# Adding the residual x with accumulating transfers from GpSimd instead of VectorE, with a new order of all work

## The chip, the cores and the metric

The kernel runs on one core of a Trainium2 chip. A core has five engines with a queue of instructions each, and every queue is worked off strictly in its order: TensorE (PE in the profile, with its weight loads as PEld), VectorE (DVE), ScalarE (ACT), GpSimd (POOL) and SyncE (SP), which here only issues transfers between the chip's main memory and the on-chip memory. Engines wait for each other by semaphores. Products of matrices land in banks of a separate small memory (PSUM), from which VectorE and ScalarE take them.

The metric is the device time of one execution in microseconds. Three runs of the kernel before gave 566.79, 567.97 and 567.18 us, a median of 567.18 us. One further execution was recorded by the hardware profiler: it took 566.9 us, and its span, from the first to the last instruction, is 564.8 us.

## The reference

The input x has 2048 tokens of 512 numbers. All is in 32-bit floats, and the result is x + s * g.

```python
xn = layernorm(x)                       # over the 512, eps 1e-5
q, k, v = split(xn @ wqkv)              # 32 heads of 16
phi = lambda t: where(t > 0, t + 1, exp(t)) + 1e-6
kv = einsum("bhsd,bhse->bhde", phi(k), v); z = phi(k).sum(tokens)
o = (phi(q) @ kv) / (phi(q) @ z + 1e-6)
s = o @ wo                              # linear attention
h = gelu(xn @ w_gate) * (xn @ w_up)     # 512 -> 1792
g = silu(h @ w_down)                    # 1792 -> 512
return x + s * g
```

## The kernel before

**The result is made transposed.** Channels lie on the 128 partitions and tokens along the rows. The output is 512 channels by 2048 tokens, cut into four chunks `c` of 512 tokens and four row tiles `n` of 128 channels: 16 output tiles of 128x512, 256 KB each. `in_A_xT` is x in the same layout.

**Precision.** A 32-bit product is made from three faster ones: each operand is split into a high part (a rounded copy, made on ScalarE by `copy`) and a low part (the difference, made on VectorE or GpSimd; `split`, L406). Large products use a scheme of seven half-size products in place of eight (`PRODUCTS`, L180), whose partial sums are seeded and taken out between products (`copy` for seeds, `out` at L1111).

**Stages.** First the tokens are normalized and k, q and the attention's sums are made (to about 140 us). At the very start, SP loads x tiles (`x0`, `x4`, `x1`, `x5`) and halves of two weights (`wk1`, `wk2`); VectorE takes the mean and variance of a tile (L552, L553, L555), GpSimd the power -1/2 (`rstd`, L557), VectorE normalizes it (`xn`, L573), TensorE transposes it (`pt`, L643), ScalarE makes its high part (`Xh`), and the first product of the main work is `k<-kq,Xh`. The high parts of the weights (`kq<-wk`) are made on ScalarE; for the later half of each weight the low part is made on GpSimd.

Then the feed-forward part runs twice over half of the tokens, `ffn(1)` for chunks 2 and 3 and `ffn(0)` for chunks 0 and 1. Its products with w_gate and w_up are `FX`, `FY`, `FZ`, those with w_down `dX`, `dY`, `dZ`; the latter are summed by VectorE into `acc` (L1119). Low parts of w_down's forms are `dl`, and for the last of seven steps they are made on GpSimd (`EASED`).

**The output tiles** (`out_tile`, L1317). For each, the gate `g` is at hand: for chunks 0 and 1 it is `acc` after `silu` on ScalarE (L1346), for chunks 2 and 3 it was stored to main memory and is loaded again into one of ten places (`SPOTS`). It is multiplied by the attention's result `s` (L1335 from a bank `sps`, L404 where `s` was stored and is loaded again, as in chunk 2), then the tile of x is added, which SP has loaded into a place of its own (`sxr`, L1326 and L1338), and SP stores the sum to `out_yT`. The chunks come in the order 2, 3, 0, 1; the last tile of all, chunk 1 with n = 3, is done in two halves of 256 tokens.

**What sets the order.** Nothing is issued where it is written. `plan.do` records each operation with what it depends on, and the list `ORDER` at the head of the file gives one permutation of all 3626 operations. They are issued in this order, and it sets what stands ahead of what in each engine's queue; semaphores then keep what depends on each other apart. `ORDER` was written out by a planner that is not part of the file. Transfers that SP issues use eight semaphores in turn, so a ninth waits until the first has landed; a store waits for its tile, and all that stands behind a waiting instruction in a queue waits with it.

## Time and profile before

| | us |
|---|---|
| median of three runs | 567.18 (566.79 to 567.97) |
| profiled execution, its own time | 566.9 |
| its span | 564.8 |
| TensorE busy | 557.8 |
| VectorE busy | 493.2 |
| ScalarE busy | 360.8 |
| GpSimd busy | 253.1 |

The span is what the profiler's rows cover; 2.1 us of the execution lie outside it. Rows of a timeline give a start from the span's begin, a duration, the engine, the line and operation with its tiles, a count where equal ones are merged, and in brackets how long the engine had been idle and what released it. A single instruction lasts longer than its distance to the next, since instructions of an engine overlap a little. The granted clock of TensorE was 0.999 of full speed.

### The profile page before, as it was taken

To read this page: it belongs to the slowest core of one execution; us is meant where nothing else is said; L and a number is where in the kernel's file an instruction comes from. 1 tells how busy PE (TensorE), PEld (TensorE's weight loads), DVE (VectorE), ACT (ScalarE), POOL (GpSimd) and SP (SyncE) were. 2 spreads that over 40 slices of the span, in tenths; PEclk is the share of its full clock that TensorE was granted. 3 is DMA by queue.
4 is the path that set the end of the run, shared out by engine and by line. 5 is a ranking of instruction groups with operands and counts; after the bars stand their busy time and mean duration, and the time that the engine had idled before them with its cause. 6 is when DMAs were issued, how large, how long until landed. Compare 5 with 4: busy or idle time off the path is not lost.

```text
span 564.8 us, 7902 instructions
## 1 busy us (share of the span) xinstructions
PE 557.8 (99%) x2630; PEld 487.0 (86%) x2630; DVE 493.2 (87%) x774; ACT 360.8 (64%) x668; POOL 253.1 (45%) x237
## 2 busy tenths in 40 slices
PE   8999999999999999999999999999999999999997
PEld 6888888888888888888888888888888888888886
DVE  7999999987798999999888776774889989898997
ACT  5987898877677876564536467867555636354730
POOL 4656677757786876431251940430413212314200
PEclk9999999999999999999999999999999999999999
DMA  7378967879978668158867998696757475778776
GB/s 266 104 217 273 274 203 233 255 223 322 352 241 300 240 234 339 43 201 311 265 233 216 389 339 335 239 344 254 243 187 242 173 247 194 233 228 286 239 247 239
DMA packets 78952, 141.29 MB, mean 250 GB/s; under 512 B 4672, under 2 KB 47680, under 8 KB 74944
## 3 DMA queue, kind: packets, MB, share of 16 engines
q1 hardware_dynamic: 78912, 140.79, 72.9%
q8 instruction: 21, 0.34, 0.2%
q14 instruction: 19, 0.16, 0.1%
HBM read 87.82 MB, written 52.95 MB: 249 GB/s over the span
## 4 chain that ended last, share of the span: by engine, by line
PE 91%; DVE 5%; DMA 2%; issue 1%; SPq 1%; ACT 0%; DVEq 0%; ACTq 0%
PE FX L442 26%; PE FZ L442 13%; PE dX L442 12%; PE gps L442 7%; PE FY L442 6%; PE dY L442 6%; PE X L442 6%; PE sps L442 4%; PE dZ L442 3%; PE Z L442 3%; PE q L442 2%; PE k L442 2%; PE Y L442 1%; DVE acc L1119 1%; PE pt L643 1%; DMA wk<-in_A_wqkv 1%
## 5 line engine op out<-in xcount | busy, mean ns | idle before, releaser
L442 PE MATMUL FX<-Xh,w 128*128 128x512 f32 x448 | 125.4, 379 | 0.0
L442 PEld LDWEIGHTS FX<-Xh,w 128*128 128x128 f32 x448 | 84.7, 189 | 12.0
L404 POOL TENSOR_TENSOR sums<-draw 128x256 f32<-128x256 f32 x28 | 26.5, 951 | 109.6 <-DVE dl L404 56.3
L1165 POOL TENSOR_TENSOR h<-h,g 128x512 f32<-128x512 f32 x28 | 39.5, 1411 | 65.9 <-DVE h L404 64.2
L442 PE MATMUL FX<-Xl,w 128*128 128x512 f32 x224 | 66.0, 379 | 0.0
L442 PE MATMUL FZ<-Xh,w 128*128 128x512 f32 x224 | 64.4, 379 | 0.0
L398 ACT COPY dY<-dX 128x512 f32<-128x512 f32 x56 | 32.1, 573 | 46.2 <-DVE acc L1119 28.4
L398 ACT COPY fu<-FX 128x512 f32<-128x512 f32 x56 | 32.7, 585 | 23.3 <-PE FX L442 19.4
L442 PEld LDWEIGHTS FX<-Xl,w 128*128 128x128 f32 x224 | 42.3, 189 | 6.0
L442 PEld LDWEIGHTS FZ<-Xh,w 128*128 128x128 f32 x224 | 42.3, 189 | 6.0
L398 ACT CAST hfh<-sums 128x512 fp32r<-128x512 f32 x56 | 34.5, 619 | 14.3 <-DVE sums L404 14.3
L442 PE MATMUL dX<-hfh,dh 128*128 128x512 f32 x112 | 41.9, 380 | 0.1
L442 PE MATMUL dX<-hfl,dh 128*128 128x512 f32 x112 | 41.5, 380 | 0.0
L442 PE MATMUL dX<-hfh,dl 128*128 128x512 f32 x112 | 41.0, 379 | 0.0
L1119 DVE TENSOR_TENSOR acc<-acc,dY 128x512 f32<-128x512 f32 x48 | 32.7, 681 | 8.9 <-PE dY L442 8.7
L404 DVE TENSOR_TENSOR hfl<-sums,hfh 128x512 fp32r<-128x512 f32 x56 | 40.2, 728 | 0.1
L404 POOL TENSOR_TENSOR tmp<-raw 128x256 f32<-128x256 f32 x28 | 29.1, 1049 | 20.1 <-DVE we L404 10.6
L1119 DVE TENSOR_TENSOR acc<-acc,dX 128x512 f32<-128x512 f32 x48 | 32.7, 683 | 5.5 <-PE dX L442 5.2
L960 POOL TENSOR_TENSOR qz<-qz,zq 128x512 f32<-128x512 f32 x16 | 23.3, 1456 | 23.1 <-DMA qz<-q_d 18.3
L442 PE MATMUL FY<-Xh,w 128*128 128x512 f32 x112 | 33.1, 379 | 0.0
L442 PE MATMUL FZ<-Xl,w 128*128 128x512 f32 x112 | 33.0, 379 | 0.0
L404 DVE TENSOR_TENSOR hfl<-h,hfh 128x512 fp32r<-128x512 f32 x42 | 32.2, 774 | 0.6 <-ACT hfh L398 0.6
(222 smaller groups left out, 1517.7 us busy)
## 6 DMA issues: line engine op xcount, KB each, us to landing
w<-w_d SPq DMA_DIRECT2D x17, 1792.0 KB, 7.9
w_d<-w SPq DMA_DIRECT2D x11, 1792.0 KB, 8.8
draw<-in_B_w_down SPq DMA_DIRECT2D x14, 512.0 KB, 4.0
w_d<-we SPq DMA_DIRECT2D x18, 256.0 KB, 2.2
x<-in_A_x SPq DMA_DIRECT2D x16, 256.0 KB, 3.3
q_d<-qp SPq DMA_DIRECT2D x16, 256.0 KB, 3.7
qz<-q_d SPq DMA_DIRECT2D x16, 256.0 KB, 3.1
q<-q_d SPq DMA_DIRECT2D x16, 256.0 KB, 3.8
```

Source lines behind the costliest of these rows:

```text
L398: do("ACT", act(n, src.psum), lambda o, i: nc.scalar.copy(o, i), dst, src, name=name)
L404: do(eng, c, lambda o, p, q: getattr(e, f"tensor_{op}")(o, p, q), dst, a, b, name=name)
L442: nc.tensor.matmul(o if r is None else o[:, r], a, turned(b), start=first, stop=made == self.passes[r], skip_group_check=self.on or r is n ...
L643: nc.tensor.transpose(o[:, k, :], a[:, j * P:(j + 1) * P], b)
L960: do("POOL", pool(D), lambda o, z: nc.gpsimd.tensor_mul(o, o, z.unsqueeze(1).to_broadcast([P, KT, P])), rows_of(q), zq, name="u")
L1119: do("DVE", dve(D), lambda o, i: nc.vector.tensor_add(o, o, i), o, ps, name="acc")
L1165: do("POOL", pool(NC), lambda o, i: nc.gpsimd.tensor_mul(o, o, i), h, g, name="h")
```

## The change

For the 12 tiles of chunks 2, 3 and 0 the load of x by SP and the addition by VectorE are gone. After the multiplication GpSimd issues a transfer with `accum_op=ALU.add`, which reads the tile of x from main memory and adds it to the tile `g` in place; SP's store waits for it. Chunk 1 is left as it was. So VectorE has 12 instructions fewer, SP 12 loads fewer, GpSimd 12 transfers more, and TensorE's products and ScalarE's work are the same in number: 2602 and 670 rows with merged ones counted apart, in both. The places `SPOTS` now hold only gates and `s`. `ORDER` is another list throughout, of 3614 operations. Lines of the changed kernel stand one lower up to L1323, and seven or eight higher behind the new lines.

```diff
 ORDER = [
-    ...
+    ...
 ]
@@ def out_tile(c, n, ps):
             else:
                 g = U("g", SPOTS, f"g{c}{n}")
                 dma(g, g_d(4 * (c - 2) + n, at(c - 2, n)), 256)
+            if c in ADDED:
+                if ps.psum:
+                    do("DVE", dve(NC), lambda o, i: nc.vector.tensor_mul(o, o, i), g, ps)
+                else:
+                    tt("DVE", "mul", g, g, ps, NC)
+                do("POOL", 1.0, lambda o, i: nc.gpsimd.dma_start(o, i, accum_op=ALU.add), g, ext(xT[rows, cols]), lat=2.6, kb=256, name="add")
+                dma(ext(outT[rows, cols]), g, 256)
+                return
             xr = U(*(("xr", FREED) if c == CHUNKS[-1] else ("g", SPOTS)), f"sxr{c}{n}")
             dma(xr, ext(xT[rows, cols]), 256)
@@
     CHUNKS = [2, 3, 0, 1]
+    ADDED = (2, 3, 0)
```

Three places of the order are shown. Names end in a running number of the buffer; what stands ahead of it is the program's name (`sps03`: chunk 0, n = 3; `acc0_1`: the tile that holds n = 2 and n = 3 of chunk 0; `acc0_2` and `acc0_3`: chunk 1; `x4` is the second tile that is normalized).

SP's queue at its very begin, before:

```order
L394 DMA x0_97<-in_A_x 128x512
L394 DMA wk1_113<-in_A_wqkv 128x512
L394 DMA wk2_119<-in_A_wqkv 128x512
L394 DMA x4_121<-in_A_x 128x512
L394 DMA x1_123<-in_A_x 128x512
L394 DMA x5_125<-in_A_x 128x512
L394 DMA wk2_119<-in_A_wqkv 128x512
L394 DMA wk1_113<-in_A_wqkv 128x512
```

The same place of SP's queue now:

```order
L393 DMA wk1_98<-in_A_wqkv 128x512
L393 DMA x0_119<-in_A_x 128x512
L393 DMA x1_121<-in_A_x 128x512
L393 DMA wk2_123<-in_A_wqkv 128x512
L393 DMA x4_125<-in_A_x 128x512
L393 DMA x5_127<-in_A_x 128x512
L393 DMA wk2_123<-in_A_wqkv 128x512
L393 DMA wk1_98<-in_A_wqkv 128x512
```

The first tile of x comes second instead of first, behind a weight tile, and the first tile of `wk2` fourth instead of third; the seventh and eighth loads are the same. In GpSimd's queue the subtraction for that weight tile now stands ahead of the first `rstd`; before, it stood behind it.

The end of GpSimd's queue, before:

```order
L404 TENSOR_TENSOR sums0_3878<-draw0_6_5230,sums0_3878 128x256
L404 TENSOR_TENSOR dl0_6_5442<-draw0_6_5230,dh0_6_5431 128x512
L404 TENSOR_TENSOR dl3_6_5467<-sums0_3878,dh3_6_5459 128x512
L404 TENSOR_TENSOR dl5_6_5486<-sums0_3878,dh5_6_5476 128x512
L404 TENSOR_TENSOR dl2_6_5538<-draw0_6_5230,dh2_6_5533 128x256
```

The end of GpSimd's queue now, but for its last six rows:

```order
L1329 DMA g21_5460<-in_A_xT 128x512
L403 TENSOR_TENSOR dl3_6_5524<-sums0_3853,dh3_6_5515 128x512
L403 TENSOR_TENSOR dl5_6_5536<-sums0_3853,dh5_6_5531 128x512
L403 TENSOR_TENSOR dl2_6_5562<-draw0_6_5245,dh2_6_5555 128x256
L1329 DMA g32_5486<-in_A_xT 128x512
L1329 DMA g30_5497<-in_A_xT 128x512
L1329 DMA g23_5418<-in_A_xT 128x512
L1329 DMA g22_5578<-in_A_xT 128x512
```

Behind these stand six more accumulating transfers; the last of all is that of `acc0_1` for chunk 0, n = 3. Two (`g20`, `g21`) stand ahead of the `dl3`, `dl5` and `dl2` that TensorE needs.

The end of VectorE's queue, before:

```order
L1335 TENSOR_TENSOR acc0_2_4124<-acc0_2_4124,sps11_5753 128x512
L404 TENSOR_TENSOR acc0_1_4195<-acc0_1_4195,sxr03_5696 128x512
L404 TENSOR_TENSOR acc0_2_4124<-acc0_2_4124,sxr11_5740 128x512
L404 TENSOR_TENSOR acc0_0_4080<-acc0_0_4080,sxr00_5718 128x512
L1335 TENSOR_TENSOR acc0_3_4142<-acc0_3_4142,sps12_5774 128x512
L404 TENSOR_TENSOR acc0_3_4142<-acc0_3_4142,sxr12_5690 128x512
L1335 TENSOR_TENSOR acc0_2_4124<-acc0_2_4124,sps10_5675 128x512
L404 TENSOR_TENSOR acc0_2_4124<-acc0_2_4124,sxr10_5750 128x512
L1333 TENSOR_TENSOR acc0_3_4142<-acc0_3_4142,sps131_5800 128x256
L404 TENSOR_TENSOR acc0_3_4142<-acc0_3_4142,sxr13_5645 128x256
L1333 TENSOR_TENSOR acc0_3_4142<-acc0_3_4142,sps130_5812 128x256
L404 TENSOR_TENSOR acc0_3_4142<-acc0_3_4142,sxr13_5645 128x256
```

The end of VectorE's queue now:

```order
L1340 TENSOR_TENSOR acc0_3_4187<-acc0_3_4187,sps130_5741 128x256
L1118 TENSOR_TENSOR acc0_1_4223<-acc0_1_4223,dX06_1_5633 128x512
L1342 TENSOR_TENSOR acc0_2_4170<-acc0_2_4170,sps11_5693 128x512
L1326 TENSOR_TENSOR acc0_1_4223<-acc0_1_4223,sps03_5593 128x512
L403 TENSOR_TENSOR acc0_2_4170<-acc0_2_4170,sxr11_5747 128x512
L403 TENSOR_TENSOR acc0_3_4187<-acc0_3_4187,sxr13_5675 128x256
L1342 TENSOR_TENSOR acc0_3_4187<-acc0_3_4187,sps12_5725 128x512
L403 TENSOR_TENSOR acc0_3_4187<-acc0_3_4187,sxr12_5553 128x512
L1342 TENSOR_TENSOR acc0_2_4170<-acc0_2_4170,sps10_5779 128x512
L403 TENSOR_TENSOR acc0_2_4170<-acc0_2_4170,sxr10_5714 128x512
L1340 TENSOR_TENSOR acc0_3_4187<-acc0_3_4187,sps131_5799 128x256
L403 TENSOR_TENSOR acc0_3_4187<-acc0_3_4187,sxr13_5675 128x256
```

The last stores in SP's queue, before:

```order
L394 DMA out_yT<-acc0_0_4080 128x512
L394 DMA out_yT<-acc0_1_4195 128x512 x2
L394 DMA out_yT<-acc0_2_4124 128x512
L394 DMA out_yT<-acc0_0_4080 128x512
L394 DMA out_yT<-acc0_3_4142 128x512
L394 DMA out_yT<-acc0_2_4124 128x512
L394 DMA out_yT<-acc0_3_4142 128x256 x2
```

The last stores in SP's queue now:

```order
L393 DMA out_yT<-acc0_0_4091 128x512
L393 DMA out_yT<-acc0_2_4170 128x512
L393 DMA out_yT<-acc0_3_4187 128x256
L393 DMA out_yT<-acc0_3_4187 128x512
L393 DMA out_yT<-acc0_1_4223 128x512
L393 DMA out_yT<-acc0_2_4170 128x512
L393 DMA out_yT<-acc0_3_4187 128x256
```

The multiplication for chunk 0, n = 3 (`sps03`) stands fourth of the last twelve on VectorE, right behind the last sum into that tile (`dX06_1`). Its store is the third from the end in SP's queue and now waits for the accumulating transfer; before, those four tiles of chunk 0 were finished by VectorE. On TensorE, 24 products of 512 columns and 16 of 256 now stand behind the last of `dX06_1`, and 20 and 12 behind the last of `sps11`.

287 rows, old and new, of the table ORDER are left out of this document.

## The prediction

> **What bounds the kernel now.** I read the page first (span, busy times, slices, chain), then the table of stretches, then the timelines of both ends.
>
> ```profile
> span 564.8 us, 7902 instructions
> PE 557.8 (99%) x2630; PEld 487.0 (86%) x2630; DVE 493.2 (87%) x774; ACT 360.8 (64%) x668; POOL 253.1 (45%) x237
> PE 91%; DVE 5%; DMA 2%; issue 1%; SPq 1%; ACT 0%; DVEq 0%; ACTq 0%
> ```
>
> The chain of waits is TensorE's for 91%. VectorE has 5%, all near the end, so an edit that unloads VectorE there looks well aimed. But a chain follows one of several tight paths; whether TensorE would end sooner without VectorE is seen only in its idle time, by stretch.
>
> ```profile
> 0.00:40.00 40.00, 37.24 (x185) 31.91 (x186) 35.18 (x69) 30.43 (x57) 23.71 (x30) 1.00 0.63 199
> 40.00:80.00 40.00, 39.97 (x197) 34.57 (x196) 37.83 (x67) 32.59 (x62) 25.22 (x23) 1.00 0.85 255
> 80.00:120.00 40.00, 40.00 (x187) 35.00 (x187) 38.39 (x58) 35.72 (x68) 29.34 (x27) 1.00 0.74 228
> ...
> 200.00:240.00 40.00, 39.91 (x185) 34.65 (x184) 38.45 (x58) 24.64 (x48) 25.15 (x25) 1.00 0.58 214
> ...
> 280.00:320.00 40.00, 39.86 (x185) 34.39 (x184) 33.46 (x53) 21.45 (x40) 21.30 (x17) 1.00 0.77 275
> ...
> 520.00:540.00 20.00, 20.00 (x94) 17.50 (x94) 19.11 (x31) 13.81 (x25) 4.41 (x4) 1.00 0.79 260
> 540.00:565.00 25.00, 20.86 (x109) 18.41 (x107) 21.51 (x37) 4.10 (x7) 0.00 (x0) 0.98 0.69 239
> ```
>
> First column after the length: TensorE's busy time, third: VectorE's. The stretches left out have 40.00. From 40 to 540 us TensorE idles 0.03 + 0.09 + 0.14 = 0.26 us, and from 540 it works without a gap until 560.86. VectorE is close behind it (19.11 of 20). Since the change leaves TensorE's products as they are, only three things can move: the start, what little stalls there are or will be between, and the 564.8 - 560.86 = 3.9 us behind the last product.
>
> **The change part by part. Removed from VectorE.**
>
> ```profile
> L404 DVE TENSOR_TENSOR g<-g,sxr 128x512 f32<-128x512 f32 x8 | 5.3, 687 | 0.0
> 548.06 1.90 DVE L404 TENSOR_TENSOR g<-g,sxr 128x512 f32<-128x512 f32 x3
> 549.17 1.89 PE L442 MATMUL sps<-pql,Mh 128*128 128x512 f32 x8
> ```
>
> Three additions take 1.90 us and each lasts 0.69, so they follow each other by (1.90 - 0.69) / 2 = 0.60. Twelve are 12 x 0.60 = 7.2 us of VectorE's last 50. TensorE covers them: it has no gap here to give back. The value of the removal is therefore 0, and the part of the 3.9 us that depends on it is looked at next. From the third row, eight products in 1.89, each lasting 0.38: one every 0.216 us.
>
> **The last 3.9 us.**
>
> ```profile
> 558.91 1.95 PE L442 MATMUL sps<-pqh,Mh 128*128 128x256 f32 x16
> 560.01 0.41 DVE L1333 TENSOR_TENSOR acc<-acc,sps 128x256 f32<-128x256 f32 x1
> 560.46 0.42 DVE L404 TENSOR_TENSOR acc<-acc,sxr 128x256 f32<-128x256 f32 x1
> 560.90 0.42 DVE L1333 TENSOR_TENSOR acc<-acc,sps 128x256 f32<-128x256 f32 x1
> 561.35 0.42 DVE L404 TENSOR_TENSOR acc<-acc,sxr 128x256 f32<-128x256 f32 x1
> 553.77 8.37 SPq L394 DMA_DIRECT2D out_yT<-acc  x9
> ```
>
> The last multiplication starts 0.04 us behind the last product, so VectorE is not late any more when TensorE ends: multiply, add, store (561.77 to the end) is a fixed chain, and it stays, as chunk 1 is not edited. With E the end of the last product, the last store is issued at about E + 0.9.
>
> What is new is the store ahead of it. SP now issues, as its last three, the store of chunk 0 n = 3, which waits for the last accumulating transfer, and then two of chunk 1. When is that transfer issued? Behind `dX06_1` stand 24 full and 16 half products: 24 x 0.216 + 16 x 0.108 = 6.9 us before E. On VectorE `sps130` comes first (its products end 0.43 later; it takes 0.41), so the sum into the tile runs from E - 6.0 to E - 5.4; then ScalarE's silu:
>
> ```profile
> 552.57 0.63 ACT L1346 ACTIVATE acc<-acc 128x512 f32<-128x512 f32 x1 [0.57 <-DVE acc L1119]
> sxr<-in_A_xT SPq DMA_DIRECT2D x5, 256.0 KB, 3.2
> out_yT<-acc SPq DMA_DIRECT2D x7, 256.0 KB, 2.6
> DMA to landing us min/median/max: 2.8/3.7/7.7
> DMA packets 78952, 141.29 MB, mean 250 GB/s; under 512 B 4672, under 2 KB 47680, under 8 KB 74944
> ```
>
> Silu ends at about E - 4.65 and the multiplication by `sps03`, 0.68 long, at E - 3.95. Let L be the time from there until the sum has landed. SP then issues three stores, 0.45 apart (nine with waits took 8.37; the three loads at the start below took 1.39): the last at E - 3.95 + L + 0.9. It is late if that is over E + 0.9, so for **L above 3.95 us**, and by as much as L is above it. No row shows such a transfer. Below, L cannot be better than a plain store near the end, 2.6; above, I take the slowest load of x, 7.7 (last row but one: all 16). The nearest row is the load of x in the last 20 us, 3.2; the sum also reads its destination, another 262 KB, which at the mean of 250 GB/s is 1.05 us. 3.2 + 1.05 = 4.25: the end moves by **0.3** (0 to 3.75).
>
> The Trainium skill, "DMA: Bandwidth & Descriptors", section on the anatomy of a transfer on the GpSimd path, gives 2.0 us plus bytes / 436 GB/s, and about 1 us more to write the descriptors: an estimate of 1.0 + 2.0 + 0.6 = 3.6 us. By it this term is 0 and the sum below is lower by 0.3; no run here shows it yet.
>
> The other eleven have room: the first two matter most. `g20`'s place is loaded anew with `g33`, behind accumulation, store and load; counted as above, `g20` is multiplied by E - 35.5 and `g33` is used at E - 17.4, so 18 us less a store and a load (3.9 median for `g`'s, twice) leave 10 for L.
>
> **GpSimd's queue.** `g20` and `g21` stand ahead of three low parts that TensorE needs.
>
> ```profile
> 522.06 3.24 POOL L404 TENSOR_TENSOR dl<-sums,dh 128x512 fp32r<-128x512 f32 x2 [1.95 <-ACT dh L398]
> L394 SPq DMA_DIRECT2D g<-g_d x8: 319/423/430, 510.7 to 538.5; - x8
> DMA to landing us min/median/max: 2.3/3.9/5.6
> ```
>
> `g21`'s multiplication ends by E - 33.7; even if GpSimd needs a whole 1.6 us, as for one of these subtractions, to issue it, `dl3` is ready at E - 30.5, and its product stands at E - 26.5. Hidden with 4 us to spare.
>
> **The start.** A new order begins with another order of loads.
>
> ```profile
> 2.17 1.39 SPq L394 DMA_DIRECT2D x<-in_A_x  x3
> 3.42 0.69 DVE L552 BATCH_NORM_STATS2 st<-x 128x6 f32<-128x512 f32 x1 [2.36 <-DMA x<-in_A_x]
> 4.22 0.62 ACT L398 CAST kq<-wk 128x512 fp32r<-128x512 f32 x1 [2.15 <-DMA wk<-in_A_wqkv]
> 4.60 0.56 POOL L557 TENSOR_TENSOR rstd<-ve,neg_half 128x1 f32<-128x1 f32 x1 [2.27 <-DVE ve L555]
> 5.12 2.68 POOL L404 TENSOR_TENSOR kq<-wk,kq 128x512 fp32r<-128x512 f32 x2
> 5.19 1.48 DVE L573 TENSOR_SCALAR xn<-x,mv,rstd 128x512 f32<-128x512 f32 x1 [0.68 <-POOL rstd L557]
> 5.42 0.62 ACT L398 CAST kq<-wk 128x512 fp32r<-128x512 f32 x1 [0.58 <-DMA wk<-in_A_wqkv]
> 6.73 0.66 PE L643 MATMUL pt<-blk,xn 128*128 128x128 f32 x4 [1.25 <-DVE xn L573]
> 7.94 1.16 PE L442 MATMUL k<-kq,Xh 128*128 128x512 f32 x4
> 8.68 1.31 ACT L398 CAST kq<-wk 128x512 fp32r<-128x512 f32 x2 [0.61 <-DMA wk<-in_A_wqkv]
> 9.28 0.54 DVE L573 TENSOR_SCALAR xn<-x,mv,rstd 128x512 f32<-128x512 f32 x1
> 9.35 0.48 PE L442 MATMUL k<-kq,Xh 128*128 128x512 f32 x1 [0.25 <-ACT kq L398]
> ```
>
> Before, the first loads land at 3.42, 4.22 and 5.42. Now the weight tile has 3.42 and x 4.22, 0.8 later. `rstd` was due 4.60 - 3.42 = 1.18 behind x: now 5.40. GpSimd's subtraction for the weight stands ahead of it, from 3.42 + 0.62 = 4.04 to 4.04 + 1.34 = 5.38: no wait. `rstd` ends at 5.96. Before, the normalization lasted 1.48, as GpSimd's subtraction ran beside it; alone it lasts 0.54 (at 9.28). Now the second subtraction waits for a tile that comes fourth, behind 5.42, and its cast, so the normalization runs alone and ends at about 6.6, as before (6.67). So the 0.8 is paid back by the collision that goes, and the first product stays near 7.9. The seventh load, for which TensorE waits until 9.35, is the same. Behind it ScalarE has a copy between its two casts (0.55 later), and TensorE fills part of that with transposes brought forward (0.41 each): **+0.2**, between -0.5 (both waits there, 0.25 each, go) and +0.8 (the swap is not paid back).
>
> **Between.** No gain above 0.26 is there. A loss is open: VectorE is busy 38.4 of 40 us in two of the stretches above, and one instruction put ahead of one that TensorE waits for costs 0.60. Four such places would be 2.4, none 0. Before has under half of one in 500 us, so I take **+0.3**, the size of what it has, between -0.3 and +2.4.
>
> **Sum,** against the profiled execution: 566.9 + 0.3 + 0.2 + 0.3 = 567.7. The median of the runs is 0.28 above that execution, so **568.0 us**: no change, where 0.2% (1.1 us) is about what a measurement of this kernel tells from none.
>
> **The rivals.** *A busier order stalls TensorE (slower).* For it: VectorE at 96% in the middle, and 0.26 us of gaps is a state with little left to improve and much to lose. Against: VectorE's work there is no more than before. With three or four places of 0.60, 1.8 to 2.4 in place of 0.3: 569.5 to 570.
>
> *The last accumulating transfer is slow (slower).* Place: third store from the end of SP's queue; from L = 3.95 each microsecond is one of the end. For it: loads of x took up to 7.7. Against: few transfers are left at that time. At 7.7, 568.0 - 0.3 + 3.75 = 571.4. The Trainium skill, "SBUF — State Buffer", section on the two sides, warns that descriptor writing on GpSimd starves while VectorE runs in its two-port mode, 620 ns becoming some 3100; it names copies, and the rows here are TENSOR_TENSOR, which no run here has shown beside such a transfer.
>
> *VectorE did hold the end (faster).* For it: the chain names VectorE from 541 on. Against: TensorE has no gap there. What can be won in all is the waits at the start (1.25 and 0.25) and the 0.26 between: 567.2 - 1.8 = 565.4.
>
> That the change doesn't do what it says is excluded by the order: 12 transfers stand on GpSimd and 12 additions are missing on VectorE.
>
> **How the numbers follow.** No change, 50%; stalls between, 25%; a late landing, 13%; faster, 12%. The forecast's own range is 566.1 to 568.3. Eight in ten needs most of the stalls and no more than the edge of the rest: 566.2 to 570.6. Faster by over 0.2% is the last rival alone, 0.12; slower the two slow ones, 0.38; within 0.2% 0.50.
>
> **What would show it.** Right: TensorE's busy time within 0.5 of 557.8, no idle stretch over 0.5 behind 16 us, the first `k` product between 7.4 and 8.7, VectorE's busy time near 493 - 12 x 0.68 = 485, and the last store issued 0.9 behind the last product or up to 0.3 later. Wrong: a wait of TensorE for VectorE or GpSimd of 0.6 or more between 16 and 560 us, or SP waiting at the third store from the end for over 0.5 us behind E. A span that shrinks by over 1.1 us would show a slack at the start that I don't see.

## The result, and the profile after

The changed kernel takes **570.97 us** (median; 569.78 to 571.38) against 567.33 us (566.79 to 567.97) of the kernel before, run beside it: a ratio of 1.0059, 95% interval 1.0043 to 1.0075. It is slower by 0.6%, three times what a measurement of this kernel can tell. The profiled execution took 570.96 us, its span is 569.1, 4.3 more than before.

The page of the changed kernel, first lines and shares of the chain of waits:

```profile
span 569.1 us, 7898 instructions
PE 558.8 (98%) x2630; PEld 488.0 (86%) x2630; DVE 494.1 (87%) x762; ACT 361.5 (64%) x668; POOL 259.1 (46%) x249
PE 88%; DVE 5%; DMA 4%; issue 1%; ACT 0%; SPq 0%; POOL 0%; DVEq 0%; ACTq 0%; POOLq 0%
```

VectorE has 12 instructions fewer and is as busy as before. TensorE's share of the chain fell by 3 points and that of the DMA engines doubled. The last product ends at 562.66 in place of 560.86, and behind it the span goes on for 6.44 us in place of 3.94. So 1.8 us are lost while TensorE still has work, and 2.5 us behind it.

**The middle.** The stretches of the changed kernel (after the length: busy time of TensorE, its weight loads, VectorE, ScalarE, GpSimd; then the granted clock, the share of the 16 DMA engines, GB/s), and the groups of TensorE's instructions between 16 and 560 us that waited for 0.3 us or more:

```profile
200.00:240.00 40.00, 40.00 (x187) 35.04 (x186) 38.00 (x57) 24.94 (x50) 25.81 (x25) 1.00 0.46 176
240.00:280.00 40.00, 39.36 (x183) 34.12 (x181) 38.06 (x62) 23.28 (x43) 6.32 (x6) 1.00 0.67 237
280.00:320.00 40.00, 38.83 (x176) 33.01 (x177) 34.67 (x49) 18.97 (x36) 22.01 (x18) 1.00 0.77 267
320.00:360.00 40.00, 40.00 (x187) 35.01 (x187) 28.27 (x44) 21.87 (x40) 13.45 (x14) 1.00 0.91 353
L441 PE MATMUL FZ<-Xh,w 128*128 128x512 f32 x224 | 65.1, 379 | 0.9 <-DMA w<-w_d 0.9
L441 PE MATMUL dX<-hfl,dh 128*128 128x512 f32 x112 | 41.1, 380 | 0.5 <-DVE hfl L403 0.5
L441 PE MATMUL dY<-hfh,dh 128*128 128x512 f32 x56 | 21.3, 381 | 0.3 <-ACT dY L397 0.3
```

Up to 240 us the new order is even a little better: by 254 us TensorE is 0.54 us ahead of the kernel before. Then it waits for a weight tile (at 279 us), for a low part from VectorE (285) and for a copy by ScalarE (295), and all of it is some 250 us ahead of the first accumulating transfer. SP's queue in that place, now and before:

```profile
269.62 0.43 SPq L393 DMA_DIRECT2D t_d<-sums  x1
270.15 0.44 SPq L393 DMA_DIRECT2D w<-w_d  x1
275.09 0.32 SPq L393 DMA_DIRECT2D q<-q_d  x1
```

```profile
264.53 1.16 SPq L394 DMA_DIRECT2D t_d<-sums  x1
265.80 0.58 SPq L394 DMA_DIRECT2D w<-w_d  x1
272.54 0.32 SPq L394 DMA_DIRECT2D q<-q_d  x1
```

The weight tile that TensorE waits for (`w12`) is asked for 4.35 us later than before, as it stands behind q loads and t stores of the turning steps, which VectorE does about 6 us later in the new order (the first transposition of the second half at 263.24 in place of 257.23).

**The tail.** The changed kernel: the last transfer in the chain of waits, VectorE and SP near the end, GpSimd's last transfer, and the DMA queues and issues between 525 and 572 us (MB, share of 16 engines; median us to landing):

```profile
554.69 7.01 DMA sxr<-in_A_xT
557.97 0.69 DVE L1326 TENSOR_TENSOR acc<-acc,sps 128x512 f32<-128x512 f32 x1
561.80 1.03 DVE L403 TENSOR_TENSOR acc<-acc,sxr 128x512 f32<-128x512 f32 x2 [3.15 <-DMA sxr<-in_A_xT]
565.84 0.42 DVE L403 TENSOR_TENSOR acc<-acc,sxr 128x256 f32<-128x256 f32 x1
553.70 2.09 SPq L393 DMA_DIRECT2D sxr<-in_A_xT  x2
559.06 0.89 POOL L1329 DMA_DIRECT2D acc<-in_A_xT  x1 [5.13 <-DVE acc L1326]
q0 software_dynamic: 1728, 3.15, 39.3%
g<-in_A_xT POOLq DMA_DIRECT2D x8, 256.0 KB, 6.1
sxr<-in_A_xT SPq DMA_DIRECT2D x4, 256.0 KB, 6.9
acc<-in_A_xT POOLq DMA_DIRECT2D x4, 256.0 KB, 6.1
```

VectorE waits 3.15 us for the last x tile of chunk 1 (`sxr11`), whose load takes 7.01 us; all that is left to do stands behind this addition in its queue, so its last instruction ends at 566.26, 3.6 us behind the last product in place of 0.9. The accumulating transfers land 6.1 us from their issue (median). The last of them, for chunk 0, n = 3, lands 5.23 us after its issue at 559.06, which is 1.63 us behind the last product. Why everything is slow here is seen in the stretches from 525 us, before and now:

```profile
525.00:545.00 20.00, 20.00 (x94) 17.53 (x93) 19.11 (x31) 11.95 (x21) 1.36 (x2) 1.00 0.79 253
545.00:565.00 20.00, 15.86 (x86) 14.03 (x84) 16.51 (x29) 2.41 (x4) 0.00 (x0) 0.97 0.71 247
```

```profile
525.00:545.00 20.00, 20.00 (x95) 17.50 (x94) 19.67 (x31) 10.30 (x18) 9.95 (x10) 1.00 0.93 251
545.00:565.00 20.00, 17.66 (x94) 15.62 (x92) 13.41 (x23) 5.37 (x10) 4.48 (x6) 1.00 1.02 261
```

The DMA engines' share (last column but one) goes from 0.79 and 0.71 to 0.93 and 1.02, while the bytes per second stay nearly the same (253 and 247, then 251 and 261 GB/s). The share adds up the time of all packets and divides it by the stretch and by 16 engines; packets overlap (up to 23 were in flight at once here), so it can pass 1. By this measure the engines are full, and not with more bytes.

### The profile page after: what moved, and what is told of

Read it like the earlier page. It is cut to its first block, busy times and chain, and to the rows that moved or that the text cites. A ratio compares the mean times of both kernels' runs of the same rounds, so it can differ in the third digit from the quotient of the medians.

```text
span 569.1 us, 7898 instructions
## 1 busy us (share of the span) xinstructions
PE 558.8 (98%) x2630; PEld 488.0 (86%) x2630; DVE 494.1 (87%) x762; ACT 361.5 (64%) x668; POOL 259.1 (46%) x249
## 3 DMA queue, kind: packets, MB, share of 16 engines
q0 software_dynamic: 1728, 3.15, 3.2%
## 4 chain that ended last, share of the span: by engine, by line
PE 88%; DVE 5%; DMA 4%; issue 1%; ACT 0%; SPq 0%; POOL 0%; DVEq 0%; ACTq 0%; POOLq 0%
PE FX L441 23%; PE dX L441 11%; PE FZ L441 11%; PE gps L441 7%; PE sps L441 6%; PE dY L441 6%; PE FY L441 6%; PE X L441 5%; PE Z L441 3%; PE dZ L441 3%; PE q L441 2%; PE k L441 2%; PE Y L441 1%; DMA sxr<-in_A_xT 1%; DMA t_d<-sums 1%
## 5 line engine op out<-in xcount | busy, mean ns | idle before, releaser
L1164 POOL TENSOR_TENSOR h<-h,g 128x512 f32<-128x512 f32 x28 | 41.5, 1486 | 38.0 <-DVE h L403 31.4
L403 DVE TENSOR_TENSOR hfl<-sums,hfh 128x512 fp32r<-128x512 f32 x56 | 41.6, 747 | 2.3 <-ACT hfh L397 2.2
L403 DVE TENSOR_TENSOR hfl<-h,hfh 128x512 fp32r<-128x512 f32 x42 | 33.5, 800 | 0.0
L403 DVE TENSOR_TENSOR h<-fu,FZ 128x512 f32<-128x512 f32 x28 | 19.2, 685 | 13.8 <-PE FZ L441 7.7
```

Of the source, the lines that this page charges most:

```text
L403: do(eng, c, lambda o, p, q: getattr(e, f"tensor_{op}")(o, p, q), dst, a, b, name=name)
L1164: do("POOL", pool(NC), lambda o, i: nc.gpsimd.tensor_mul(o, o, i), h, g, name="h")
```

## The experiments

All runs in one table. "Last product" and "tail" (from its end to the end of the span) are of the profiled execution, one each; the ratio is to the kernel before, run beside it. Four runs leave out a part of the work and so give another result, to measure that part: noadd, plain, nostores and four. In five runs the profiled execution lies over 1 us from the median, so their last two columns carry less: noadd (570.25), oldorder (571.79), early_x (573.53), hyb1050 (570.88) and hyb1050_dve0 (574.85).

| run | median us | ratio, 95% interval | last product | tail |
|---|---|---|---|---|
| before (beside the changed kernel) | 567.33 | | 560.86 | 3.94 |
| changed kernel | 570.97 | 1.0059 [1.0043, 1.0075] | 562.66 | 6.44 |
| noadd | 569.18 | 1.0030 [1.0017, 1.0042] | 564.55 | 3.85 |
| plain | 569.00 | 1.0029 [1.0018, 1.0040] | 562.81 | 3.79 |
| oldorder | 573.87 | 1.0107 [1.0083, 1.0131] | 560.73 | 9.17 |
| w12 | 572.67 | 1.0091 [1.0074, 1.0107] | 563.88 | 6.32 |
| w12b | 573.14 | 1.0115 [1.0077, 1.0153] | 564.36 | 6.44 |
| early_x | 571.23 | 1.0073 [1.0051, 1.0095] | 564.10 | 7.60 |
| dve0 | 569.87 | 1.0043 [1.0029, 1.0058] | 563.14 | 4.36 |
| dve0_w12b | 574.05 | 1.0120 [1.0085, 1.0156] | 567.84 | 4.46 |
| turns | 578.36 | 1.0190 [1.0173, 1.0207] | 569.83 | 7.27 |
| turns_dve0 | 576.59 | 1.0167 [1.0152, 1.0182] | 570.20 | 4.40 |
| hyb700 | 574.87 | 1.0131 [1.0116, 1.0146] | 566.50 | 7.20 |
| hyb1050 | 572.37 | 1.0085 [1.0064, 1.0105] | 562.49 | 6.31 |
| hyb1050_dve0 | 570.75 | 1.0059 [1.0042, 1.0075] | 567.90 | 4.10 |
| hyb1470 | 570.86 | 1.0059 [1.0044, 1.0074] | 561.47 | 7.43 |
| hyb1470_dve0 | 568.44 | 1.0022 [1.0012, 1.0032] | 562.35 | 4.05 |
| nostores | 569.60 | 1.0034 [1.0019, 1.0049] | 563.17 | 4.53 |
| four | 569.94 | 1.0061 [1.0037, 1.0085] | 561.93 | 5.87 |

**1. Transfers away (noadd), transfers without the adding (plain).**

```diff
-                do("POOL", 1.0, lambda o, i: nc.gpsimd.dma_start(o, i, accum_op=ALU.add), g, ext(xT[rows, cols]), ...)
```

> The changed kernel without its 12 accumulating transfers: x is not added to the 12 tiles, each is stored right after its multiplication; nothing else differs, and the order of the remaining work is the changed kernel's. Theory (two losses that add up: the new order loses about 1.8 us of TensorE's time between 275 and 299 us, and the transfers lengthen the tail behind the last product by about 2.5 us): the transfer that brings the last x tile of chunk 1 lands within 3 to 4 us of its issue in place of 6.9, VectorE no longer waits 3.15 us for it, the tail behind the last product is 3.9 to 4.5 us in place of 6.4, the stalls of TensorE at 279, 285 and 295 us stay, and the time is 568.7 (568.2 to 569.2). Rival one (the transfers cost all of it, by holding the queue of SP and the DMA engines): 567.0 to 567.5, the stalls at 279 to 295 us gone. Rival two (the new order costs all of it, since it frees the place of that last x tile only 7 us ahead of the end): about 571, VectorE still waits 2 to 3 us for the x tile.

```diff
-                ... nc.gpsimd.dma_start(o, i, accum_op=ALU.add) ...
+                ... nc.gpsimd.dma_start(o, i) ...
```

> The changed kernel with the 12 transfers of GpSimd kept, in the same places, but plain: each overwrites its tile with x instead of adding to it, so 12 of 16 output tiles hold x alone. It measures what the adding itself costs. Theory (an accumulating transfer holds the DMA engines about twice as long per byte as a plain one, and this is what stretches all transfers of the tail): the 12 transfers land in 3 to 4.5 us in place of 6.1, the x tile of chunk 1 lands sooner, the tail shortens by 1 to 2 us, time 569 to 570. Rival (the length comes from GpSimd's own queue and from many transfers at once, whatever they do): landing stays near 6 us and the time within 0.4 of 571.

Both end 3.8 to 3.9 us behind the last product, as the kernel before, and both take about 569.1 us. Plain transfers of GpSimd thus cost nothing that can be measured (569.00 against 569.18); the *adding* costs 1.8 to 2.0 us. The tail of plain is 2.65 us shorter than that of the changed kernel, more than the 1 to 2 us expected. The same rows of the run with plain transfers:

```profile
q0 software_dynamic: 960, 3.15, 19.2%
g<-in_A_xT POOLq DMA_DIRECT2D x8, 256.0 KB, 4.3
acc<-in_A_xT POOLq DMA_DIRECT2D x4, 256.0 KB, 4.0
sxr<-in_A_xT SPq DMA_DIRECT2D x4, 256.0 KB, 3.6
```

For the same 3.15 MB the adding transfers hold the DMA engines 39.3% of the window of 47 us in place of 19.2%: per transfer 0.393 x 47 / 12 = 1.54 us of all 16 engines, in place of 0.75. What is left without them, 569.18 against 567.42, 1.8 us, belongs to the new order. In the profiled execution of noadd the stalls in the middle are there (0.73, 0.84 and 0.91 us from one product to the next, 0.22 without a stall), with two more at 327 and 337 us. Both rivals that give all the blame to one side fall.

**2. The old order with the transfers (oldorder).** `ORDER` of the kernel before, and in `out_tile`, for the 12 tiles of chunks 2, 3 and 0:

```diff
-            dma(xr, ext(xT[rows, cols]), 256)
-                tt("DVE", "add", o, o, xr[:, cs], w)
+                do("POOL", 1.0, lambda o, i: nc.gpsimd.dma_start(o, i, accum_op=ALU.add), g, ext(xT[rows, cols]), ...)
```

> The kernel before with the accumulating transfers alone: its own order of all work is kept, each of the 12 additions on VectorE is replaced at its place by GpSimd's accumulating transfer, and the 12 loads of x for them are left out. Theory (order and transfers each cost a part): no stall between 275 and 299 us, so the products up to 500 us run as in the kernel before; at the end stores that wait 4 to 6 us each for a transfer hold up the loads that stand behind them in SP's queue, which this order was not made for: last product 561 to 563, tail 5 to 8 us, time 568.5 to 573. Rival one (the transfers cost all, the order nothing): 571 or more with the last product late by the same 1.8 us as in the changed kernel. Rival two (the transfers cost nothing by themselves): 567.3.

No stall in the middle, last product at 560.73: the old order keeps its 500 us without loss. But the tail is 9.17 us, and the run is 2.9 us slower than the changed kernel; tail and time lie above the 5 to 8 us and the 568.5 to 573 us expected. So the new order costs 1.8 us without the transfers, and with them it is worth 2.9: it loses in the middle and gains more at the end. The last transfer of oldorder takes 7.6 us, and SP's nine last stores take 10.50 us, as some wait for transfers:

```profile
acc<-in_A_xT POOLq DMA_DIRECT2D x1, 256.0 KB, 7.6
556.28 10.50 SPq L396 DMA_DIRECT2D out_yT<-acc  x9
```

VectorE's busy time is 486.5 us here, 6.7 less than before for 12 additions less, and 7.6 us less than in the changed kernel.

**3. The late weight tile (w12, w12b).** One entry moved in SP's queue (w12: ahead of the load of q9; w12b: ahead of that of q10):

```diff
+ w12<-w_d                (w12)
  q9<-q_d
  t_d<-sums
+ w12<-w_d                (w12b)
  q10<-q_d
  t_d<-sums
- w12<-w_d
```

> The changed kernel with one entry of the order moved: the load of weight tile w12 stands in SP's queue ahead of the load of q9, four places earlier, where it waits only for the last product that reads the place it fills (about 260 us). Theory (this load, issued at 270.15 us behind two q loads and two t stores, came too late): the stall of 1.23 us ahead of the first product with w12 (at 279 us) goes, the last product ends 1.0 to 2.0 us earlier (560.7 to 561.7 in place of 562.7), the tail stays at 6.4, time 569.0 to 570.0. Rival (the products there wait for the transposed q or for h tiles of VectorE and ScalarE, and w12 only came last by chance): the stall moves to another releaser and the time stays within 0.4 of 571.

> The changed kernel with the load of weight tile w12 moved two places up in SP's queue, ahead of the load of q10 and a t store, and behind the load of q9 (the run that put it ahead of q9 as well made VectorE wait). It then issues at about 265.2 us in place of 270.15; before had 265.8. Theory (w12 came late behind a q load that waits for VectorE's sums, which this order does 5 to 6 us later): no stall ahead of the first w12 product at 279 us, and none made at 270: last product 1.0 to 2.0 us earlier, time 569.0 to 570.0. Rival (either w12 or the q tiles come late, whichever stands behind: the DMA engines or VectorE's order set it): a stall of 0.7 us or more turns up elsewhere between 268 and 300 us and the time stays at 570.6 or above.

The stall at 279 us went as expected, and one of 2.4 us (w12) or 3.1 us (w12b) came at 270 or 274 us. VectorE, in w12 and in w12b:

```profile
269.88 0.69 DVE L1225 SCALAR_TENSOR_TENSOR q<-q,rall 128x512 f32<-128x512 f32 x1 [2.48 <-DMA q<-q_d]
```

```profile
275.50 0.69 DVE L1225 SCALAR_TENSOR_TENSOR q<-q,rall 128x512 f32<-128x512 f32 x1 [3.16 <-DMA q<-q_d]
```

Now the q tile comes late behind the 1792 KB of the weight tile, VectorE waits for it, and with it all that stands behind it in VectorE's queue, for which TensorE waits. Both times lie above the 569 to 570 us of the theory, and that of w12 above its rival's 571 as well. The theory that one late load was the cause fell; the rival of w12b (whichever stands behind is late) held.

**4. The turning steps back in their old place (turns, turns_dve0).** 18 entries of the order (the first turning steps of the second half and w12's load) where the kernel before has them, counted in products.

> The changed kernel with 18 entries of the order moved back to where the kernel before has them, counted in products of TensorE: the first four turn steps of the second half (load of q, two operations on VectorE, store of t; 17 entries) and the load of w12 behind them, some 9 to 21 entries of TensorE earlier; the accumulating transfers and all else stay. Theory (this order begins the turn steps 6 us later, 263.2 in place of 257.2 us, and packs them closer, so that q loads and w12's load of 1.79 MB meet on the DMA engines; moving the load alone only moved the wait from TensorE to VectorE): the stalls at 270 to 300 us go, the last product ends 1.5 to 2.6 us earlier (560.1 to 561.2), the tail of 6.4 stays, time 568.5 to 569.6. Rival (the stalls in the middle belong to the whole new order and come elsewhere when one place is mended): last product at 562 or later, time 570.5 or more.

> The run before this one with chunk 0's four additions back on VectorE and early x loads for the last chunk, so that only eight accumulating transfers are left. Theory (two separate losses): both gone, last product 560.3 to 561.5, tail 3.9 to 4.4, time 566.6 to 567.8: the kernel before, or a little faster. Rival (middle not mended by this): 569.5 or more.

Both are the slowest of all, where at most 569.6 and 567.8 us were expected: the last product comes at 570. In turns VectorE is busy for 33.8 of the 34 us from 230 to 264, so what is put ahead there pushes back what TensorE needs: stalls of 2.85 us at 260, 2.08 at 284 and 1.41 at 300 us. That the turning steps come late is part of the new order, not by itself its fault.

**5. The two halves of the order (hyb700, hyb1050, hyb1470).** The order of the kernel before up to a point (entries of TensorE: 700, 1050, 1470; about 230, 344 and 483 us of the kernel before), then the rest in the changed kernel's order; all 12 transfers.

```diff
-ORDER                                  (the changed kernel's)
+O = ORDER of the kernel before, up to its 1470th entry of TensorE
+ORDER = O + [n for n in ORDER if n not in O]
```

> The same, but the order of the kernel before is followed only up to about 230 us; the stretch from 230 to 344 us is in the changed kernel's order. If the loss is made by the order inside this stretch (turn steps, q loads and w12 pressed together while VectorE is busy 38 of 40 us), the stalls at 270 to 340 us are there as in the changed kernel: last product 562 to 565, time 570.5 or more. If it is made by what the order ahead of 230 us leaves undone, they are gone: last product 560.3 to 561.5, time 568.8 to 570.5.

> The changed kernel with all 12 accumulating transfers, whose order follows the kernel before, entry by entry, up to about 344 us of that kernel, and the changed kernel from there on. Theory (the loss of 1.8 us in the middle is made by the new order of the stretch ahead of 344 us and by nothing else): no stall over 0.6 us ahead of 344 us, last product within 0.6 of the 560.9 of the kernel before, tail 6.0 to 7.6 as in the changed kernel, time 568.8 to 570.5. Rival (what is lost there comes back somewhere else, since the later order is built on it): last product at 562 or later, time 571 or more.

> The changed kernel with all 12 accumulating transfers, whose order follows the kernel before up to about 483 us, where VectorE and the DMA engines have room and the two orders have done nearly the same work, and the changed kernel from there on. Theory (the loss in the middle is made by the new order between 230 and 341 us; the cut at 344 us only made a loss of its own): last product within 0.6 of the 560.9 of the kernel before, tail 6.0 to 7.6, time 569.0 to 570.5. Rival (the new tail needs the new middle): last product at 562 or later, time 571 or more.

Busy time of TensorE from 230 to 345 us, in this order: before, the changed kernel, hyb700, hyb1050, hyb1470:

```profile
230.00:345.00 115.00, 114.77 (x531) 99.53 (x530) 100.17 (x157) 61.87 (x114) 44.90 (x38) 1.00 0.74 267
```

```profile
230.00:345.00 115.00, 113.20 (x521) 97.78 (x520) 101.71 (x155) 60.53 (x113) 44.03 (x39) 1.00 0.72 258
```

```profile
230.00:345.00 115.00, 111.75 (x513) 95.77 (x512) 100.19 (x154) 59.77 (x111) 43.74 (x39) 1.00 0.70 251
```

```profile
230.00:345.00 115.00, 114.82 (x531) 99.60 (x530) 100.20 (x157) 62.01 (x114) 44.53 (x38) 1.00 0.74 266
```

```profile
230.00:345.00 115.00, 114.44 (x528) 98.96 (x528) 100.03 (x157) 61.39 (x113) 44.76 (x38) 1.00 0.74 266
```

Where this stretch has the old order, 0.2 to 0.6 us of 115 are lost; where it has the new one, 1.8 and 3.25 (hyb700 has a stall of 1.05 at its cut, at 232 us, and its last product comes at 566.50, later than the 562 to 565 expected). Busy time blurs short waits, so I also took the time between the starts of the 1100th and the 1600th product. By it the new order costs against the kernel before 1.98 us in the changed kernel, 3.16 in noadd, 1.70 in plain, 1.03 in dve0, 0.81 in four and 3.04 in hyb700, the old one -0.16 in oldorder, -0.06 in hyb1050, 0.56 in hyb1470. The same order loses more or less from one execution to the next, but always something. So the loss in the middle is made by the new order *inside* 230 to 345 us. hyb1050 misses its expected time and comes out where its rival said, since the cut at 344 us makes a stall of its own (1.1 us). hyb1470 has no such cut, and still takes 570.86, 0.4 more than expected: its last product comes 1.2 us sooner than the changed kernel's, and its tail is 1.0 us longer. Mending the middle alone gains nothing.

**6. The tail: one late x tile (early_x), chunk 0 on VectorE (dve0 and its relatives).**

```diff
-            xr = U(*(("xr", FREED) ...
+            xr = U(*(("xr", (20, 21, 12, 13)) ...
  SP's queue
  sxr12<-in_A_xT
+ sxr10<-in_A_xT
  ...
  sxr13<-in_A_xT
+ sxr11<-in_A_xT
  ...
- sxr10<-in_A_xT
- sxr11<-in_A_xT
```

In dve0 the places are (20, 25, 12, 13), and for chunk 0, with x loaded by SP into places of its own:

```diff
-                do("POOL", 1.0, ... accum_op=ALU.add ...)
+                tt("DVE", "add", g, g, xr, NC)
```

> The changed kernel with all 12 accumulating transfers, but the x tiles sxr10 and sxr11 of the last chunk get two places of the h ring whose last readers come earlier (places 20 and 21 in place of 10 and 11), and their loads stand right behind those of sxr12 and sxr13 in SP's queue, at about 534 and 548 us in place of 553.7 and 554.7. Theory (the tail is longer because the place of sxr11 comes free only about 7 us ahead of the last product and its load then takes 7.0 us instead of 3.6 beside the accumulating transfers): VectorE's wait of 3.15 us goes and its last addition ends 0.9 to 1.3 us behind the last product in place of 3.6; what then ends last is the store of the last accumulated tile, third from the end of SP's queue, whose transfer is issued 3.6 us ahead of the last product and lands 5 to 6.5 us later; tail 4.8 to 6.0 in place of 6.4, time 569.3 to 570.5. Rival (the DMA engines are so full that any load or store in this stretch is late): VectorE waits somewhere else, time within 0.4 of 571.

> The changed kernel with the early x loads (sxr10 and sxr11 in places 20 and 25) and chunk 0's four additions back on VectorE, at the places where the order had the accumulating transfers, with four x loads of their own issued 533 to 548 us; only the eight transfers of chunks 2 and 3 are left. Theory (the transfers hurt by what waits for them near the end, not by being there): tail of 3.9 to 4.4 us, time 568.4 to 569.2, as in the runs without the transfers and with plain ones (569.2 and 569.0). Rival (the load on the DMA engines alone costs it): 569.7 or more, VectorE or SP waiting for loads behind 540 us.

early_x did what it should, and gained nothing. VectorE's wait for the x tile is gone and its last addition ends 0.9 us behind the last product, but SP's stores of accumulated tiles now end last. In early_x:

```profile
564.59 0.42 DVE L403 TENSOR_TENSOR acc<-acc,sxr 128x256 f32<-128x256 f32 x1
562.23 5.47 SPq L393 DMA_DIRECT2D out_yT<-acc  x8
560.49 0.89 POOL L1329 DMA_DIRECT2D acc<-in_A_xT  x1 [4.15 <-DVE acc L1326]
acc<-in_A_xT POOLq DMA_DIRECT2D x1, 256.0 KB, 5.8
```

The last transfer, issued at 560.49, lands at 566.3, and the store third from the end waits for it: the place that the prediction named. Its forecast of 4.8 to 6.0 us for the tail was missed (7.60), as the transfers became slower still (median of the four of chunk 0 7.3). This execution was the slowest of the four of early_x, 2.3 us above their median, so its tail may be longer than usual; the median of 571.23 still shows no gain. dve0 leaves only transfers that are issued ahead of 548 us, and its tail is 4.36 us; its time, 569.87, is 0.7 over the upper end that was expected and so in the range of the rival, but the tail came as the theory said; what is over is the 2.3 us lost ahead of the last product.

> The same with chunk 0's four additions back on VectorE and early x loads for the last chunk. Theory (two separate losses are all of the difference): last product within 0.9 of 560.9, tail 3.9 to 4.4, time 567.0 to 568.4, the same as the kernel before within what can be measured. Rival (eight transfers cost something by themselves): 568.8 or more.

With both losses mended the kernel takes 568.44 us, 2.4 us less than hyb1470; 0.2% [0.1, 0.3] over the kernel before remain, just over the upper end that was expected, with the last product at 562.35, of which 0.9 us were lost ahead of 210 us in the profiled execution. No version was found that beats the kernel before.

> Both edits together: chunk 0 and the early x loads as in the run before this one, and w12's load ahead of q10's. Theory (two separate losses, each with its own cure): 567.0 to 568.2, about the time of the kernel before. Rival (the stalls in the middle come in one place or another whatever is moved): 568.6 or more.

> The first of these three with chunk 0's four additions back on VectorE and early x loads for the last chunk: eight accumulating transfers are left, all issued ahead of about 550 us. Theory (the two losses are separate and these are the only ones): last product within 0.6 of 560.9, tail 3.9 to 4.4, time 567.0 to 568.3, as the kernel before. Rival: 569 or more, by a loss that neither edit takes away.

These two have a tail of 4.46 and 4.10 us as well, and the stalls of w12b and of the cut at 344 us; their times miss the expectation. A third loss is in both: VectorE waits 0.8 and 1.3 us near 555 us for one of the x loads that were added for chunk 0, and TensorE, which needs what stands behind, has a stall of 1.2 and 1.7 us near 558 us. So the cure at the end is not free of waits either.

**7. What fills the tail (nostores, four).**

For chunks 2 and 3, in nostores:

```diff
-                dma(ext(outT[rows, cols]), g, 256)
```

> The changed kernel with all 12 accumulating transfers, but the eight stores of chunks 2 and 3 left out (these 8 of 16 output tiles are never written), 2 MB less for the DMA engines between 530 and 556 us; nothing behind those stores waits for them but the place of g33 and SP's queue. In the changed kernel the DMA engines were busy 0.93 of 525 to 545 us and all of 545 to 565 us (the kernel before 0.79 and 0.71; without the transfers 0.59 and 0.51). Theory (the tail is bound by the DMA engines, which the accumulating transfers fill): the transfers and the last x loads land sooner (accumulating 4.5 to 5.5 us in place of 6.1, the x tile 4 to 5.5 in place of 7.0), tail 4.1 to 5.0 in place of 6.4, time 569.0 to 570.0. Rival (an accumulating transfer takes 6 us by itself, and the x load's 7 us comes from standing behind one): landing stays at 5.8 to 6.3 us, tail 6 or more, time within 0.4 of 571.

And in four:

```diff
-                do("POOL", 1.0, ... accum_op=ALU.add ...)
```

> The changed kernel with the four accumulating transfers of chunk 0 alone (x is not added to the eight tiles of chunks 2 and 3), the last of them as late as before. Theory (bound by the DMA engines): with a third of the added load they are not full, the four land in 3.5 to 5 us, tail 4.1 to 4.8, time 568.9 to 569.8. Rival (what counts is that the last store waits for a late accumulating transfer of 6 us): tail 6 or more and time within 0.5 of 571.

The last accumulating transfer of nostores, then of four:

```profile
acc<-in_A_xT POOLq DMA_DIRECT2D x1, 256.0 KB, 3.6
```

```profile
acc<-in_A_xT POOLq DMA_DIRECT2D x1, 256.0 KB, 4.8
```

With 2 MB of other traffic away, the twelve transfers are the same; the last lands in 3.6 us in place of 5.2, their median is 5.3 in place of 6.1, the x load of chunk 1 takes 4.81 in place of 7.01, and the tail falls to 4.53 us. So the load on the DMA engines lengthens these transfers. It is not all: in four the engines are not full (shares 0.63 and 0.75), and the late transfer still takes 4.8 us. It lands 1.15 us behind the last product, SP's last stores wait for it, and the tail is 5.87 us, longer than the 4.1 to 4.8 expected. Nor do full engines make the tail by themselves. The two stretches of dve0:

```profile
525.00:545.00 20.00, 20.00 (x94) 17.52 (x93) 19.67 (x31) 10.36 (x18) 9.13 (x9) 1.00 0.97 266
545.00:565.00 20.00, 18.07 (x94) 15.39 (x92) 16.66 (x29) 5.32 (x10) 1.76 (x3) 1.00 0.95 285
```

The shares are 0.97 and 0.95, nearly those of the changed kernel, but the last of its eight transfers lands 7.6 us ahead of the last product, and the tail is 4.36 us. The tail grows where the last instructions wait for a slow transfer: slow transfers and a late wait are both needed, and these runs do not tell how much each is worth. The two runs spread more than others (567.28 to 571.15 and 568.67 to 573.43), so their medians carry less than their rows.

## Why the prediction was wrong

It forecast 568.0 us, between 566.2 and 570.6, and gave 0.38 to slower; it came to 570.97, above the range. Two terms of its sum were too small: the last 3.9 us, put at +0.3, grew by 2.5, and the stretch between, put at +0.3, cost 1.8 by the last product. Each lies within the bounds that the prediction gave for it alone. Its two slow rivals were priced at 569.5 to 570 and at 571.4, each alone; both losses came, and the range did not have their sum.

- **What bounds the kernel: right, but one resource short.** TensorE works without a gap and the removal of 12 additions gains nothing: noadd, which has neither additions nor transfers, is slower than the kernel before. But the quoted stretches also showed the DMA engines at 0.79 and 0.69 from 520 us, and the text made nothing of it.
- **The last 3.9 us: the failed step.** The term was 0.3 (0 to 3.75) and measured 2.5. The mechanism it named, a late last transfer, is real (early_x, oldorder, four). The multiplication ended 4.0 us ahead of the last product, almost the 3.95 worked out; but L was not 4.25. GpSimd began to issue 0.4 us later and the transfer landed 5.2 after that, so L was 5.6, which by itself would have cost 5.6 - 3.95 = 1.7 us. And it was not what ended last in the changed kernel: that was VectorE's work on chunk 1 behind the load of `sxr11`, which took 7.01 us, and so the last store was issued 2.7 us later than forecast. Two sentences fail. One is that the chain of multiply, add and store "stays, as chunk 1 is not edited": its x load runs beside the new transfers. The other is "the other eleven have room": it looked at places and not at the load that all twelve put on the DMA engines. The working had the means: it counted the bytes of the destination a second time for one transfer's duration. Counted for all, as an estimate from the rows above: of 30.0 us busy (0.79 x 20 + 0.71 x 20) in the 40 us from 525, ten plain loads of x go (14 stood in this window, 4 are left; at 0.75, -7.5) and twelve transfers come (at 1.54, +18.5), which makes 41.0 us of 40. Measured are 0.93 x 20 + 1.02 x 20 = 39.0, and some of it behind 565 us.
- **"Against: few transfers are left at that time"** was the reason for 13%. It is wrong: the transfers that lengthen a late one are the eleven others and SP's stores and loads, and from 545 to 565 us the share of the DMA engines was 1.02.
- **Between: right in mechanism and range, wrong in chance and in cause.** The rival's price was 1.8 to 2.4 and 1.8 was measured, but it had 25%. The premise against it, that "VectorE's work there is no more than before", does not hold: VectorE's busy time stayed at 494.1, where 485 was forecast and oldorder, with the same 12 additions less, has 486.5. The mean of its TENSOR_TENSOR rows is 728 ns in the changed kernel and in noadd, 714 before and in oldorder. So it is the new order that makes its instructions longer, and the trace shows which: all of VectorE's 512-wide TENSOR_TENSOR rows of over 0.76 us lie beside an instruction of GpSimd, and there are 70 of them in the changed kernel and 69 in noadd, against 59 before and in oldorder. Whether the stalls of TensorE come from these is not shown. Which pair of entries in 230 to 345 us costs most stays open; three attempts to move single pieces made it worse.
- **The start: right.** First `k` product at 8.44, within the forecast of 7.4 to 8.7 but 0.5 later than the 7.9 worked out; normalization 0.53 alone in place of 1.48 beside GpSimd, as worked out. At the 80th product +0.34, and by 64 us the new order had won it back (-0.23), which was not foreseen and is small.
- **GpSimd's queue: right.** An accumulating transfer takes 0.88 us to issue there, not the 1.6 allowed, and TensorE has no gap from 520 to 545 us.
- **The places named as signs.** Idle TensorE of over 0.5 us behind 16 us: seen, at 279 us. TensorE's busy time within 0.5 of 557.8: it was 558.8. VectorE's busy time of 485: not seen. Last store 0.9 behind the last product: missed by 2.7. SP waiting at the third store from the end: not seen in the changed kernel, where VectorE was later still. The Trainium skill's fit for one transfer ("DMA: Bandwidth & Descriptors", section on the anatomy of a transfer on the GpSimd path), 2.0 us plus bytes / 436 GB/s, gives an estimate of 2.6 us for 256 KB; the 1.0 us that the prediction added for the descriptors is no term of that fit. The shortest plain transfer of GpSimd took 2.7 us (plain), the shortest accumulating ones 3.5 and 3.6 (nostores, four), and those of the changed kernel 4.0 to 7.9. The Trainium skill's warning on descriptor writing ("SBUF — State Buffer", section on the two sides) is not borne out here: in the changed kernel the issues stay at 0.87 to 1.07 us beside TENSOR_TENSOR.

## What to carry to other kernels

A transfer that adds moves its work from a compute engine to the DMA engines, and here it weighed double there (1.54 us of all engines in place of 0.75): multiply its engine time by the number of transfers and add it to the DMA share of the very stretch where they run, before looking at any single latency. An engine that is off the critical path is no place to save, and a new order of all work is a change of its own: price it apart, by running the old order with the new instructions and the new order without them. When a cure for one late wait gains nothing (early_x, hyb1470), look for a resource that is full, and then for what still waits for it at the very end: dve0, with the engines as full, has a tail of 4.36 us.

## What the hardware showed that was not expected

- An accumulating transfer of 128x512 (256 KB) from main memory into on-chip memory takes 144 packets in place of 80 (1728 and 960 for 12) and 1.54 us of all 16 DMA engines in place of 0.75. The data packets carry 2 KB each in place of 4 KB, and one takes about as long (median of all packets 178 and 159 ns). It lands in 3.6 to 4.8 us in four, where the engines have room, and in 4.0 to 7.9 in the changed kernel, where they are full. GpSimd needs 0.88 us to issue it, 0.55 for the plain one (median of twelve).
- After four of the five stalls of TensorE of over 2.6 us its clock fell to half. The run turns, behind its stall of 2.85 us at 260:

```profile
264.00:267.00 3.00, 3.00 (x8) 2.34 (x9) 2.34 (x4) 0.00 (x0) 1.27 (x1) 0.50 0.42 134
267.00:272.00 5.00, 5.00 (x24) 4.34 (x23) 4.40 (x7) 2.37 (x4) 0.00 (x0) 0.96 0.44 134
```

For about 3 us products came every 0.427 us in place of 0.216, which costs another 1.5 us. Counted from one product's start to the next, it was so behind stalls of 2.66 (hyb1050_dve0), 2.85 (turns), 2.86 (turns_dve0) and 3.67 us (dve0_w12b), and not behind one of 3.06 us (w12b). The Trainium skill, "TensorE: Matmul & The Clock Gate", Part 1, says that the clock halves after an idle window of about 3.4 us that runs freely; that a longer stall may escape fits a free window, that 2.66 us suffice is shorter than it says.
